# Two more pieces of raw weights loaded at the opening of an attention-plus-two-MLP kernel

## The chip, the cores and the metric

The kernel runs on one core of one Trainium2 chip. The metric is the device time of one execution in microseconds (us), lower is better; a time is the median of several runs.

## What is computed

Attention over pooled keys and values, then an MLP with ELU, then an MLP with a normalised softmax gate; all in float32, with products accurate to about float32.

```
k_p, v_p = k, v averaged over groups of 8 rows          # 8 batches, 8 heads, 576 rows of 64
x   = softmax(q @ k_p.T / 8) @ v_p                      # 4608 tokens x 512
h   = x @ w_in;  g = where(h > 0, h, exp(h) - 1)        # w_in 512 x 2048
x   = g @ w_out                                         # w_out 2048 x 512
h   = x @ moe2_w_in;  solu = h * softmax(h)             # 512 x 1024
out = layernorm(solu) * g_ln @ moe2_w_out               # 1024 x 512
```

The weights lie in memory as 64-bit words (float64); the kernel loads them as such and turns them into float32 on the chip. q, k and v are float32.

## The kernel before

**Blocks and slots.** The 4608 tokens form nine blocks of 512. The first MLP runs block by block; for each block, 16 slots f go through the hidden units, 128 a slot: 12 matmuls h1 (`m_h1`, L455), the ELU on VectorE (L466, L467), and 12 matmuls into the output accumulators (`m_o1`, L488). Every operand is split into a high and a low part, so each product takes three matmuls. The attention of the 32 pairs of heads is spread over the slots of the blocks ahead of where it is needed (`att_half`), apart from pairs 0 to 3, which come first, in `startup`. The second MLP follows behind the ninth block.

**Weights.** They come in pieces of two columns of 128 (`("i", c)`: w_in) or two rows of 128 (`("o", c)`: w_out), c = 0, 2, ... 14, sixteen pieces in all, in the order i0, o0, i2, o2, i4, and so on. `conv_load` (L315) loads a piece as raw 64-bit words into a tile `raw`, with two transfers of 512 KB. `conv` (L329) makes float32 of it with one instruction on ScalarE (L342) and three on VectorE (L344, L346, L348); the result of a w_in piece goes to a tile `cv` and from there, by `conv_split`, to `wh` and `wl`; that of a w_out piece goes to a half of a tile `wo`. `next_conv` converts the next piece of a list `cq` and loads the next of a list `lq`; it is called through the slots of block 0 until the list is empty, so all conversion is done by the end of block 0.

**The opening.** `startup` computes pairs 0 to 3 and converts i0 and o0. Of each pair: reduce k over groups of eight (`K`, L138), scores (L163), maximum and subtraction (L179, L188), exponential on ScalarE (L193), sum, reciprocal and product (`att_soft`, L200 to L204), transposes on TensorE (L214, L219) and copies on ScalarE (L215, L221), product with v (L238), and the split of the result into `xh` and `xl` (L251, L252), which the first h1 matmul needs beside `wh` and `wl`.

**Tiles and queues.** Three rings of tiles of 8 KB a partition matter here. Ring `x` has six: raw words, `xh`, `xl`. Ring `w` has eight, for `wh` and `wl` of four groups of slots; in the opening it holds four tiles with k and q of pairs 0 to 3 and a tile `kz`. Ring `wo` has four, for `wo`; in the opening it holds two tiles with v. All transfers are issued by SP, in one queue. A k tile of a later pair (tag `k`) has one buffer: k5's transfer waits until k4 is reduced.

**The order on each engine.** The text of the program gives the order of priority; a scheduler then lays the instructions of each engine in a queue of its own at build time, by its own idea of when operands are ready. What stands in a queue runs in that order on the chip.

Of the kernel before, what the change touches and what calls it, by code (L numbers as in the profile page):

```python
# [11 lines left out]
I64 = mybir.dt.int64  # L12
# [6 lines left out]
def kernel(  # L19
# [16 lines left out]
    P = 128  # L36
# [11 lines left out]
    sb = ctx.enter_context(tc.tile_pool(name="sb", bufs=2))  # L48
# [72 lines left out]
    def att_setup(i, what="kv"):  # L121
        b, p = units[i]
        early = i < NP
        if early:
            k_t, _, v_t = st["kq", p]
            if "kz" not in st:
                kz = sb.tile([P, 4, 512], F32, name="kz", tag="w", bufs=8)
                nc.vector.memset(kz[:, :, 0:2 * SK], 0.0)
                st["kz"] = kz
            kp = st["kz"][:, p, 0:2 * SK]  # L130
            vt = st["kz"][0:SK, p, 2 * SK:2 * SK + P]
        else:
            k_t, v_t = st.pop(("ld", i))
            kp = kpbd[i % 2]
            vt = p1.tile([SK, P], F32, name=f"vt{i}", tag="vt")
        if "k" in what:
            kr = p1.tile([P, SK], F32, name=f"kr{i}", tag="kr", bufs=1)
            nc.vector.tensor_reduce(kr, k_t.rearrange("p (s t) -> p s t", t=POOL), axis=AX, op=ALU.add)  # L138
            cpy = nc.vector.tensor_copy if early else nc.scalar.copy
            cpy(kp[0:64, 0:SK], kr[0:64, :])  # L140
            cpy(kp[64:128, SK:2 * SK], kr[64:128, :])
        if "v" in what:
            vr = p1.tile([SK, P], F32, name=f"vr{i}", tag="vr", bufs=1)
            if early:
                pool_tree(vr, v_t)
            else:
                nc.vector.tensor_reduce(vr, v_t, axis=AX, op=ALU.add)
            nc.scalar.mul(vt, vr, 1.0 / POOL)
        st["kp", b, p] = (kp, vt)
# [4 lines left out]
    def att_scores(i, banks):  # L154

        kp, vt = st["kp", units[i][0], units[i][1]]
        q_t = st.pop(("q", i))
        st["sv", i] = []
        for t0 in (0, 3):
            s = next(banks)  # L160
            ts = QT[t0:t0 + 3]
            for t, o in enumerate(ts):
                nc.tensor.matmul(  # L163
                    s[:, t * 2 * SK:(t + 1) * 2 * SK], q_t[:, o:o + P], kp, start=True, stop=True
                )
            m = 2 * len(ts)
            st["sv", i].append((2 * t0, m, s[:, 0:m * SK].rearrange("p (a k) -> p a k", k=SK)))
            yield
        st["a", i] = (p1.tile([P, NG, SK], F32, name=f"es{i}", tag="es", bufs=3), vt)

    def att_max(i):
        es, vt = st["a", i]
        mx = p1.tile([P, NG], F32, name=f"mx{i}", tag="mx", bufs=4)
        summed = NP <= i < NEXP
        if summed:
            st["sm", i] = p1.tile([P, NG], F32, name=f"sm{i}", tag="mx", bufs=4)
        for g0, m, sv in st.pop(("sv", i)):
            mxs = mx[:, g0:g0 + m]
            nc.vector.tensor_reduce(mxs, sv, axis=AX, op=ALU.max)  # L179
            if summed:  # L180
                nc.vector.tensor_scalar(mxs, mxs, -1.0 / (8 * POOL), None, op0=ALU.mult)
                for g in range(m):
                    nc.scalar.activation(
                        es[:, g0 + g, :], sv[:, g, :], AF.Exp, bias=mx[:, g0 + g:g0 + g + 1],
                        scale=1.0 / (8 * POOL), accum_out=st["sm", i][:, g0 + g:g0 + g + 1],
                    )
            else:
                nc.vector.tensor_tensor(es[:, g0:g0 + m, :], sv, bc(mxs, m), op=ALU.subtract)  # L188

    def att_exp(i):  # L190
        es, vt = st["a", i]
        if ("sm", i) not in st:
            nc.scalar.activation(es, es, AF.Exp, scale=1.0 / (8 * POOL))  # L193
# [31 lines left out]
    def att_V(i, banks):  # L225


        b, p = units[i]
        es, vt = st.pop(("a", i))
        a = st.pop(("aT", i))  # L230
        j = b * S // 512
        n = 512 * (j + 1) - b * S
        st["pv", i] = []
        for o, w, blk, at in ((0, n, j, b * S - 512 * j), (n, S - n, j + 1, 0)):
            pv = next(banks)
            for h in range(2):
                d = slice(64 * h, 64 * h + 64)
                nc.tensor.matmul(pv[d, 0:w], vt[:, d], a[:, h, o:o + w], start=True, stop=True)  # L238
            st["pv", i].append((pv[:, 0:w], blk, slice(at, at + w)))
# [24 lines left out]
    def double():  # L264
        t = ps.tile([P, 2, 512], F32, name="at2", tag="A")
        yield t[:, 0]
        yield t[:, 1]
# [34 lines left out]
    for j in range(NBLK):  # L302
        i = ((starts[j] + sizes[j] - 1) // S) * NP + NP - 1
# [8 lines left out]
    wraw, wcv, wh, wl, wo = {}, {}, {}, {}, {}  # L312
    w2, o2h, o2l = {}, {}, {}

    def conv_load(key):  # L315
        kind, i = key
        raw = sb.tile([P, 2, 512], I64, name="raw", tag="x", bufs=6)
        for a in range(2):
            c, d = i + a, raw[:, a, :]
            if kind == "i":  # L320
                nc.sync.dma_start(
                    out=d.rearrange("p (k f) -> p k f", k=KDM),
                    in_=w_in[:, c * P:(c + 1) * P].rearrange("(k p) f -> p k f", p=P),
                )
            else:
                nc.sync.dma_start(out=d, in_=w_out[c * P:(c + 1) * P, :])
        wraw[key] = raw

    def conv(key):  # L329
        kind, i = key  # L330
        raw = wraw.pop(key).bitcast(U32).rearrange("p a f -> p (a f)")
        hw, lw = raw[:, 1::2], raw[:, 0::2]
        if kind == "o":
            if i % 4 == 0:
                wo[i // 4] = sb.tile([P, 4, 512], F32, name="wo", tag="wo", bufs=4)
            w2 = wo[i // 4][:, i % 4:i % 4 + 2, :]
        else:
            w2 = sb.tile([P, 2, 512], F32, name="cv", tag="cv", bufs=2)
        w = w2.rearrange("p a f -> p (a f)")
        wu = w.bitcast(U32)  # L340
        wcv[key] = w2
        nc.scalar.activation(w, hw.bitcast(F32), AF.Abs, scale=2.0**-112)  # L342
        yield
        nc.vector.tensor_scalar(wu, wu, 3, None, op0=ALU.logical_shift_left)  # L344
        yield
        nc.vector.scalar_tensor_tensor(wu, lw, 29, wu, op0=ALU.logical_shift_right, op1=ALU.bitwise_or)  # L346
        yield
        nc.vector.scalar_tensor_tensor(wu, hw, 0x80000000, wu, op0=ALU.bitwise_and, op1=ALU.bitwise_or)  # L348
        yield
# [295 lines left out]
    lq = list(order)  # L645
    cq = list(order)

    def next_load():
        if lq:
            conv_load(lq.pop(0))  # L650
# [16 lines left out]
    def startup():  # L667

        ci, co = conv(("i", 0)), conv(("o", 0))

        def K(i):
            att_setup(i, "k")

        def S_(i):
            for _ in att_scores(i, double()):
                pass

        def M(i):
            att_max(i)
            att_exp(i)  # L680

        def V(i):
            att_setup(i, "v")
            att_V(i, double())

        def T(i):
            att_T(i, 0)
            att_T(i, 1)

        K(0)  # L690
        S_(0)
        K(1)
        S_(1)
        M(0)
        K(2)
        M(1)
        S_(2)
        K(3)
        att_soft(0)
        T(0)  # L700
        M(2)
        S_(3)
        att_soft(1)
        T(1)
        M(3)
        V(0)
        next(ci)
        att_soft(2)
        T(2)
        V(1)  # L710
        att_x(0)
        next(ci)
        next(ci)
        att_soft(3)
        T(3)
        att_x(1)
        V(2)
        next(ci)
        conv_split(("i", 0))
        att_x(2)  # L720
        V(3)
        att_x(3)
        for _ in co:
            pass
        conv_split(("o", 0))

    with tc.manual_schedule():
        for i in range(NP):
            att_load(i, "kq")
        att_load(0, "v")  # L730
        att_load(1, "v")
        conv_load(("i", 0))
        att_load(2, "v")
        att_load(3, "v")
        conv_load(("o", 0))
        startup()
    del cq[:2], lq[:2]
    next_load()
    nload[0] = NP
    step = 4 * NP  # L740
    while nload[0] < NP + 2:
# [124 lines left out]
```

## Time and profile before

| | |
|---|---|
| median of 3 runs | 1401.44 us (1400.01 to 1404.63) |
| the profiled execution's own time | 1404.09 us |
| its span | 1402.3 us |
| TensorE matmul busy | 1344.3 us, 96% |
| VectorE (DVE) busy | 863.5 us, 62% |
| ScalarE (ACT) busy | 649.1 us, 46% |
| GpSimd (POOL) busy | 302.9 us, 22% |
| mean granted TensorE clock | 0.985 |

The span is counted from the first to the last instruction; start times in the rows are from its beginning. A bracket in a row of the timeline gives the time that the engine sat idle ahead of the instruction and what ended it. SPq is SP's queue; a transfer's row there is its issue, not its run.

### The profile page before, as it was taken

The numbers are of one execution on the slowest core, as the hardware profiler recorded it, in microseconds if no ns is written. First come the engines' busy times: TensorE is split into PE (matmuls) and PEld (weight loads), VectorE is DVE, ScalarE is ACT, GpSimd is POOL, SyncE is SP. The second block draws the span as 40 slices with busy tenths as digits, with TensorE's granted clock in tenths as the row PEclk, the third lists the DMA queues.
The fourth block names the chain that finished last, engine by engine and source line by source line (L and its number), as shares of the span: only waits on it lengthen the run. The fifth ranks groups of instructions, "written<-read, shape, count | busy, mean of one in ns | idle before, by whom it ended". The sixth has DMA issues, their size and how long they took to land.

```text
span 1402.3 us, 16772 instructions
## 1 busy us (share of the span) xinstructions
PE 1344.3 (96%) x6260; PEld 1070.7 (76%) x6260; DVE 863.5 (62%) x1470; ACT 649.1 (46%) x1257; POOL 302.9 (22%) x245
## 2 busy tenths in 40 slices
PE   4698999999999999999999999999899999999998
PEld 3366778878788788787787777887688888787876
DVE  6699966566566466555554375643857575656653
ACT  2555544444444344444444343433645464555443
POOL 2245422222322222222223132221000000000000
PEclk7699999999999999999999999999999999999999
DMA  7355321122022122121010141535111101110000
GB/s 211 105 173 174 113 94 64 35 94 73 26 94 73 28 92 73 35 64 35 27 38 1 33 177 61 188 142 207 41 53 53 41 36 53 53 53 24 26 20 38
DMA packets 48336, 105.93 MB, mean 76 GB/s; under 512 B 4608, under 2 KB 12800, under 8 KB 46848
## 3 DMA queue, kind: packets, MB, share of 16 engines
q1 hardware_dynamic: 48256, 104.88, 22.5%
q8 instruction: 49, 0.80, 0.2%
q14 instruction: 31, 0.25, 0.1%
HBM read 74.45 MB, written 30.41 MB: 75 GB/s over the span
## 4 chain that ended last, share of the span: by engine, by line
PE 75%; DVE 14%; DMA 5%; ACT 3%; issue 2%; POOL 0%; SPq 0%; DVEq 0%; ACTq 0%
PE o L488 24%; PE h L455 24%; PE po L632 9%; PE xy L549 7%; DVE e L599 2%; PE z L549 2%; PE at L163 2%; DMA x1r<-x1d 2%; PE at L238 2%; PE pt L214 2%; DVE sc L595 1%; DMA k<-in_k 1%; ACT ha L605 1%; DMA raw<-in_w 1%; PE pt L617 1%
## 5 line engine op out<-in xcount | busy, mean ns | idle before, releaser
L437 POOL TENSOR_TENSOR wol<-wo,woh 128x512 fp32r<-128x512 f32 x144 | 205.2, 1425 | 535.2 <-ACT woh L436 535.2
L455 PE MATMUL h<-xh,wh 128*128 128x512 f32 x576 | 236.8, 411 | 1.0 <-ACT wh L362 1.0
L488 PE MATMUL o<-gh,woh 128*128 128x512 f32 x576 | 228.0, 396 | 7.4 <-ACT woh L436 5.0
L488 PE MATMUL o<-gh,wol 128*128 128x512 f32 x576 | 227.2, 394 | 1.8 <-POOL wol L437 1.8
L455 PE MATMUL h<-xl,wh 128*128 128x512 f32 x576 | 227.1, 394 | 0.0
L455 PE MATMUL h<-xh,wl 128*128 128x512 f32 x576 | 225.9, 392 | 0.5 <-POOL wl L363 0.5
L632 PE MATMUL po<-o,dhl 128*128 128x512 f32 x864 | 209.4, 394 | 2.0 <-ACT dhl L620 2.0
L466 DVE TENSOR_SCALAR e<-e 128x512 f32<-128x512 f32 x144 | 62.9, 437 | 220.7 <-ACT e L460 220.4
L632 PEld LDWEIGHTS po<-o,dhl 128*128 128x128 f32 x864 | 161.3, 188 | 37.3 <-ACT dhl L620 2.5
L460 ACT ACTIVATE e<-h 128x512 f32<-128x512 f32 x144 | 86.1, 598 | 214.1 <-PE h L455 214.1
L469 ACT CAST gh<-e 128x512 fp32r<-128x512 f32 x144 | 89.6, 622 | 154.1 <-DVE e L467 154.1
L455 PEld LDWEIGHTS h<-xh,wh 128*128 128x128 f32 x576 | 108.6, 189 | 34.7 <-issue 13.6
L488 PEld LDWEIGHTS o<-gh,woh 128*128 128x128 f32 x576 | 108.9, 189 | 33.0 <-ACT woh L436 5.5
L488 PEld LDWEIGHTS o<-gh,wol 128*128 128x128 f32 x576 | 108.9, 189 | 25.8 <-POOL wol L437 2.3
L455 PEld LDWEIGHTS h<-xl,wh 128*128 128x128 f32 x576 | 108.4, 188 | 24.9
L455 PEld LDWEIGHTS h<-xh,wl 128*128 128x128 f32 x576 | 108.9, 189 | 21.9 <-POOL wl L363 1.4
L436 ACT CAST woh<-wo 128x512 fp32r<-128x512 f32 x144 | 89.4, 622 | 35.4 <-PE o L488 32.4
L607 POOL TENSOR_TENSOR sc<-sc,mhalf 128x1 f32<-128x1 f32 x36 | 21.5, 596 | 389.9 <-DVE sc L606 389.9
L467 DVE TENSOR_TENSOR e<-e,h 128x512 f32<-128x512 f32 x144 | 98.9, 687 | 3.7
L549 PE MATMUL xy<-T,xh 128*128 128x512 f32 x216 | 78.0, 402 | 1.6 <-DVE ha L572 0.9
L635 ACT ACTIVATE ot<-po,sc 128x512 f32<-128x512 f32 x36 | 24.7, 687 | 86.1 <-PE po L632 79.0
L204 POOL TENSOR_TENSOR es<-es,sm 128x720 f32<-128x720 f32 x28 | 41.2, 1472 | 100.5 <-DVE sm L202 92.4
(562 smaller groups left out, 2207.0 us busy)
## 6 DMA issues: line engine op xcount, KB each, us to landing
raw<-in_w SPq DMA_DIRECT2D x48, 512.0 KB
v<-in_v SPq DMA_DIRECT2D x32, 288.0 KB
x1d<-x1s SPq DMA_DIRECT2D x9, 1024.0 KB
x1r<-x1d SPq DMA_DIRECT2D x9, 1024.0 KB
out<-ot SPq DMA_DIRECT2D x36, 256.0 KB
k<-in_k SPq DMA_DIRECT2D x28, 288.0 KB
q<-in_q SPq DMA_DIRECT2D x28, 288.0 KB
w2d<-cv SPq DMA_DIRECT2D x14, 512.0 KB
```

The lines of the kernel that those rows point to most:

```text
L163: nc.tensor.matmul(s[:, t * 2 * SK:(t + 1) * 2 * SK], q_t[:, o:o + P], kp, start=True, stop=True)
L204: eng.tensor_tensor(es, es, bc(sm, NG), op=ALU.mult)
L436: nc.scalar.copy(oh, t[:, f % 4, :])
L437: nc.gpsimd.tensor_tensor(ol, t[:, f % 4, :], oh.bitcast(F32), op=ALU.subtract)
L455: nc.tensor.matmul(h[:, 0:n], a[g][:, kk, fo:fo + P], x[j][:, kk, 0:n], start=(i == 0), stop=(i == 3 * KDM - 1))
L460: nc.scalar.activation(e[:, 0:n], h[:, 0:n], AF.Exp)
L466: nc.vector.tensor_scalar(e[:, 0:n], e[:, 0:n], 1.0, 1.0, op0=ALU.min, op1=ALU.subtract)
L467: nc.vector.tensor_tensor(e[:, 0:n], e[:, 0:n], h[:, 0:n], op=ALU.max)
L469: nc.scalar.copy(gh[:, 0:n], e[:, 0:n])
L488: nc.tensor.matmul(acc, a[:, dm * P:(dm + 1) * P], x[:, 0:n], start=(f == 0 and m == 0), stop=(f == NF - 1 and m == 2))
L549: nc.tensor.matmul(bank, x[:, o:o + P], w[:, y + k, :], start=(start and m == 0), stop=(stop and m == 5), skip_group_check=True,)
L632: nc.tensor.matmul(po, a[:, c, :], w[c // 4][:, c % 4, :], start=(m == 0), stop=(m == 3 * NC2 - 1))
```

## The change

The list of loads moves by two pieces. The raw words of i2 and o2 are loaded in the opening, right behind those of o0: i2 into a tile of ring `w`, o2 into a tile of ring `wo`, and the load that followed the opening (`next_load()`) goes. The list of conversions stays as it was, so loads run two pieces further ahead of conversions. Lines of the changed kernel from `conv_load` on are two higher, those behind the opening three.

```diff
     def conv_load(key):
         kind, i = key
-        raw = sb.tile([P, 2, 512], I64, name="raw", tag="x", bufs=6)
+        tag, bufs = {("i", 2): ("w", 8), ("o", 2): ("wo", 4)}.get(key, ("x", 6))
+        raw = sb.tile([P, 2, 512], I64, name="raw", tag=tag, bufs=bufs)
...
         conv_load(("o", 0))
+        conv_load(("i", 2))
+        conv_load(("o", 2))
         startup()
-    del cq[:2], lq[:2]
-    next_load()
+    del cq[:2], lq[:4]
     nload[0] = NP
```

What it does to the queues is more than the diff shows. On SP's queue, from the second pair of v tiles (v22) on; raw_105, raw_110, raw_113 and raw_116 are the words of i0, o0, i2 and o2; k4, q4, v4 and q5 belong to pairs 4 and 5. Before:

```order
L112 DMA v22_97<-in_v 72x1024 x2
L326 DMA raw_110<-in_w2 128x512 x2
L107 DMA k4_351<-in_k 128x576
L109 DMA q4_353<-in_q 128x576
L112 DMA v4_352<-in_v 72x1024
L109 DMA q5_359<-in_q 128x576
L107 DMA k5_357<-in_k 128x576
```

And now:

```order
L112 DMA v22_97<-in_v 72x1024 x2
L328 DMA raw_110<-in_w2 128x512 x2
L323 DMA raw_113<-in_w1 128x4x128 x2
L328 DMA raw_116<-in_w2 128x512 x2
L107 DMA k4_354<-in_k 128x576
L109 DMA q4_356<-in_q 128x576
L112 DMA v4_355<-in_v 72x1024
L109 DMA q5_362<-in_q 128x576
L107 DMA k5_360<-in_k 128x576
```

Four transfers of 512 KB stand ahead of k4. On ACT, from the exponential of pair 0 (es0) on, before:

```order
L193 ACTIVATE es0_125<-es0_125 128x720
L193 ACTIVATE es1_136<-es1_136 128x720
L215 COPY a0_169<-pt0_0_170 72x512
L215 COPY a0_169<-pt0_1_176 72x512
L221 COPY a0_169<-pr0_182 72x2x64
L193 ACTIVATE es2_159<-es2_159 128x720
```

And now; L344 is L342 of before, here for o2, and kpbd0, kpbd1 belong to pairs 4 and 5:

```order
L193 ACTIVATE es0_131<-es0_131 128x720
L344 ACTIVATE wo_348<-raw_116 128x1024
L193 ACTIVATE es1_142<-es1_142 128x720
L140 COPY kpbd0_77<-kr4_367 64x72
L141 COPY kpbd0_77<-kr4_367 64x72
L215 COPY a0_175<-pt0_0_176 72x512
L140 COPY kpbd1_78<-kr5_550 64x72
L141 COPY kpbd1_78<-kr5_550 64x72
L215 COPY a0_175<-pt0_1_182 72x512
```

The conversion of o2 stands ahead of the exponential of pair 1. On DVE, from the subtraction of pair 1 (es1) on, before:

```order
L179 TENSOR_REDUCE mx1_147<-at2_130 128x4
L188 TENSOR_TENSOR es1_136<-at2_130,mx1_147 128x288
L138 TENSOR_REDUCE kr3_160<-kq3_100 128x72
L140 COPY kz_113<-kr3_160 64x72
L141 COPY kz_113<-kr3_160 64x72
L200 TENSOR_REDUCE sm0_164<-es0_125 128x10
L201 TENSOR_SCALAR sm0_164<-sm0_164 128x10
L202 RECIPROCAL sm0_164<-sm0_164 128x10
L204 TENSOR_TENSOR es0_125<-es0_125,sm0_164 128x720
L179 TENSOR_REDUCE mx2_186<-at2_153 128x6
```

And now; L346, L348 and L350 are L344, L346 and L348 of before:

```order
L179 TENSOR_REDUCE mx1_153<-at2_136 128x4
L346 TENSOR_SCALAR wo_348<-wo_348 128x1024
L188 TENSOR_TENSOR es1_142<-at2_136,mx1_153 128x288
L138 TENSOR_REDUCE kr3_166<-kq3_100 128x72
L348 SCALAR_TENSOR_TENSOR wo_348<-raw_116,wo_348 128x1024
L140 COPY kz_119<-kr3_166 64x72
L141 COPY kz_119<-kr3_166 64x72
L200 TENSOR_REDUCE sm0_170<-es0_131 128x10
L138 TENSOR_REDUCE kr4_367<-k4_354 128x72
L201 TENSOR_SCALAR sm0_170<-sm0_170 128x10
L350 SCALAR_TENSOR_TENSOR wo_348<-raw_116,wo_348 128x1024
L202 RECIPROCAL sm0_170<-sm0_170 128x10
```

The three steps for o2 and the reduction of k4 have moved in among the work of pairs 0 and 1; those for i2 follow further down, ahead of the rest of i0's. From the reduction of pair 9's v (vr9, the 180th instruction of DVE in both) all queues are the same.

## Rows read from the trace of the kernel before

**Rows 1.** The page: busy time and share of the span.
```profile
PE 1344.3 (96%) x6260; PEld 1070.7 (76%) x6260; DVE 863.5 (62%) x1470; ACT 649.1 (46%) x1257; POOL 302.9 (22%) x245
```
**Rows 2.** Stretches (us), length, then each engine's busy time, PEclk, DMA share, GB/s.
```profile
0.00:155.00 155.00, 112.08 (x488) 82.33 (x488) 128.93 (x171) 79.36 (x207) 58.51 (x51) 0.87 0.55 170
145.00:155.00 10.00, 7.11 (x32) 4.79 (x30) 9.97 (x14) 7.01 (x28) 3.06 (x3) 1.00 0.62 214
155.00:180.00 25.00, 24.99 (x123) 19.28 (x124) 21.72 (x29) 12.53 (x27) 13.49 (x9) 1.00 0.12 36
```
**Rows 3.** Waits of DVE from 13 to 156 us: total, times, longest.
```profile
DVE xl L252 <- ACT xh L251: 6.5, 5, 3.4
DVE kr L138 <- DMA k<-in_k: 5.8, 2, 4.7
DVE vr L147 <- DMA k<-in_k: 2.9, 1, 2.9
DVE wo L344 <- ACT wo L342: 1.2, 1, 1.2
DVE gl__940 L476 <- ACT gh L469: 0.7, 1, 0.7
DVE gl__468 L476 <- ACT gh L469: 0.6, 1, 0.6
DVE cv L344 <- ACT cv L342: 0.5, 1, 0.5
DVE mx L179 <- PE at L163: 0.5, 1, 0.5
```
**Rows 4.** Timeline of the opening: start, duration, instruction.
```profile
13.70 0.46 DVE L188 TENSOR_TENSOR es<-at,mx 128x288 f32<-128x288 f32 x1
...
27.97 0.75 DVE L138 TENSOR_REDUCE kr<-k 128x72 f32<-128x576 f32 x1 [4.67 <-DMA k<-in_k]
...
50.44 1.16 PE L455 MATMUL h<-xh,wh 128*128 128x512 f32 x2 [0.97 <-ACT wh L362]
```
**Rows 5.** Timeline of SP's queue: start of the issue and its length.
```profile
13.84 0.33 SPq L107 DMA_DIRECT2D k<-in_k  x1
...
20.98 0.33 SPq L109 DMA_DIRECT2D q<-in_q  x1
28.75 7.81 SPq L107 DMA_DIRECT2D k<-in_k  x3
```
**Rows 6.** Stretches of three us in the opening, columns as in Rows 2.
```profile
6.00:9.00 3.00, 2.98 (x12) 2.99 (x13) 1.32 (x4) 0.00 (x0) 0.00 (x0) 1.00 1.00 376
9.00:12.00 3.00, 1.78 (x10) 1.56 (x8) 2.88 (x7) 0.80 (x1) 0.00 (x0) 1.00 1.08 262
12.00:15.00 3.00, 1.46 (x10) 1.28 (x10) 2.87 (x7) 0.81 (x1) 1.11 (x1) 1.00 1.07 278
15.00:18.00 3.00, 0.00 (x0) 0.00 (x0) 2.85 (x6) 0.00 (x0) 2.76 (x5) 0.84 1.08 282
18.00:21.00 3.00, 1.78 (x9) 1.35 (x10) 2.93 (x5) 0.58 (x1) 0.31 (x1) 0.50 0.97 218
```
**Rows 7.** DMA issues: transfers and size of one.
```profile
raw<-in_w SPq DMA_DIRECT2D x48, 512.0 KB
...
k<-in_k SPq DMA_DIRECT2D x28, 288.0 KB
```
**Rows 8.** Timeline: conversion steps on ACT and DVE in block 0.
```profile
58.92 1.17 ACT L342 ACTIVATE wo<-raw 128x1024 f32<-128x1024 f32 x1
58.98 0.69 DVE L344 TENSOR_SCALAR cv<-cv 128x1024 uint32<-128x1024 uint32 x1 [0.54 <-ACT cv L342]
...
72.15 1.88 DVE L344 TENSOR_SCALAR wo<-wo 128x1024 uint32<-128x1024 uint32 x1
74.06 1.22 DVE L346 SCALAR_TENSOR_TENSOR wo<-raw,wo 128x1024 uint32<-128x1024 uint32 x1
75.32 1.22 DVE L348 SCALAR_TENSOR_TENSOR wo<-raw,wo 128x1024 uint32<-128x1024 uint32 x1
```

## The prediction

> **What bounds the kernel now.** I began with the page's busy time. TensorE (PE) is busy for 96% of the span [rows 1], so what a change is worth is how much idle time of PE it adds or takes away. The stretches tell where that idle time lies: before 155 us PE is busy for 112.08 of 155, behind it 24.99 of 25 [rows 2]. In the same first stretch VectorE (DVE) is busy for 128.93 us, and in its last ten us for 9.97, while PE has 7.11 [rows 2]. So DVE bounds the time up to about 155 us, by attention of the first pairs, ELU and conversion, and PE everything behind it. The waits of DVE from 13 us on are the third view: 18.7 us in eight kinds, the sum of the totals of [rows 3], with the transfer of k4 the largest single one, 4.67 us at 27.97 [rows 3, 4]. The fourth is the order of the queues, since that is what the change moves.
>
> One thing makes the sum simple. DVE executes the same instructions in both kernels, and from vr9 on all queues are equal. So the whole difference is made by that point, and it is the change in DVE's idle time up to there (and in how long its instructions take), as long as DVE is the bound.
>
> **What it removes, adds and moves.** No arithmetic is added. The four transfers of i2 and o2 come earlier, in the opening; the later loads move up by two pieces; conversion of o2 and i2 moves from block 0 into the opening. None of the two early tiles waits for a free place: ring `wo` has two tiles with v and the first `wo` beside o2, ring `w` seven tiles beside i2 until i2 is converted.
>
> *The stall.* ACT now has o2's conversion second, behind the exponential of pair 0, and DVE has the first step on its result ahead of es1's second part. That part starts at 13.70 before [rows 4]. Now everything behind it waits on both engines until o2's words have landed and ACT has converted them, and PE with them, for the transposes of pair 0 need DVE's product. When do they land? Before, the transfers of k4, q4, v4 and q5 are issued between 13.84 and 20.98 [rows 5]; each takes its turn when an older one has landed. In the new order these four turns belong to i2 and o2. k4 landed at 27.97, where DVE's wait for it ended [rows 4]: by then all of the opening up to o0 was there. In front of the end of o2 now lie four transfers of 512 KB more, and k4's 288 KB no longer [rows 7]: 2.10 MB less 0.295 is 1.80 MB. From 9 to 18 us, when the DMA engines are as full as they get, they move 262, 278 and 282 GB/s [rows 6], 274 on average. That is 1.80 / 0.274 = 6.6 us, so o2 lands at 34.5. The bounds are the fastest and slowest of the full rows, 376 and 218 GB/s [rows 6]: 4.8 and 8.3 us, 32.8 and 36.2. I take the average, since i2 comes in pieces of 1 KB as i0 did, and i0 was under way in these rows. ACT's step takes 1.17 [rows 8]. DVE goes on at 34.5 + 1.17 = 35.7 in place of 13.70: **+22.0 us** of idle time (20.3 to 23.7).
>
> A page speaks of a faster rate: the Trainium skill, DMA: Bandwidth & Descriptors, section Bandwidth, has 1 MB from memory arriving at 341 GB/s. By it the 1.80 MB would take 5.3 us and the sum below would be an estimated 1.3 us less. The rows above show less in this opening, and are used.
>
> *What the stall takes in.* k4 lands 288 KB behind o2, some 1.1 us later at 274 GB/s, and its reduction now stands seven DVE instructions behind the point where DVE resumes, so its wait of 4.67 goes. k5's, the other part of the 5.8 of that row [rows 3], goes too: its transfer can start when k4 is reduced, and a conversion step, the product of pair 0 and a maximum now lie between. **-5.8**. The waits of DVE on ACT's first conversion step, 1.2 and 0.5 [rows 3], come from words that landed late or a full ACT; with loads two pieces ahead I count them as gone: **-1.7**. The wait of 2.9 at vr and those of xl on xh, 6.5, hang on POOL, ACT and PE in the chain behind pairs 2 and 3, which is ordered as before; they stay. Bounds: only k4's 4.7 goes, or all 18.7.
>
> *The conversions themselves.* In block 0 o2's three steps took 1.88, 1.22 and 1.22 [rows 8]; the first ran beside POOL's subtractions. In the opening POOL waits too, and I take 0.69 for it, what the same step took for i2, undisturbed [rows 8]: **-1.2** (0 to -1.2). i2's three take the same as before. The work on DVE is only moved, so it gives no more than this. That conversions are out of the way when the first slots run is of use to PE, which can run slot 2 while o0 is converted, but DVE is what bounds that stretch, and PE's gain there is waited away later.
>
> *SP.* k4, q4, v4, q5 are issued four turns later; their readers stand behind the stalled instructions, so this costs nothing, as long as DVE resumes after o2. Loads of i4 and o4 wait for the same releases of ring `x` as i2 and o2 did (the last steps of i0 and o0), and are needed two pieces later: nothing.
>
> *Sum:* 22.0 - 5.8 - 1.7 - 1.2 = **+13.3 us**. Against the profiled execution's own 1404.09 that is 1417.4; this execution was 2.65 above the median of its three runs, 1401.44, so the median to expect is **1414.7 us**. The first h1 matmul, at 50.44 before [rows 4], shifts by more than the end does: by the stall less k4's and k5's waits, plus the two conversions now ahead of it, 0.69 + 1.22 + 1.22 = 3.1 us each [rows 8]: 22.0 - 5.8 + 6.2, so about 73 us; block 0 gives the conversions back.
>
> **The rivals.** *The idle time is nearly all made good.* After a long stall nothing is late any more, and DVE never waits again. For it: 18.7 us of waits are there to be taken in [rows 3]. Against it: 9.4 of them, xl and vr, end with work that is itself behind the stall. It gives 22.0 - 18.7 - 1.2 = +2.1, 1403.5.
>
> *New waits in the opening.* The reductions of k5 and k6 now stand among the instructions of pairs 0 to 2 on DVE, and ACT copies k5's result between two copies of pair 0, so both queues now wait for a chain of load, reduce, load that they had behind them before. SP's three issues k5, k6, k7 take 7.81 us in one row [rows 5], so a link of it takes about (7.81 - 0.33) / 2 = 3.7. I find enough work between the links to cover one; where both are uncovered by three quarters, it costs 5.6 more: +18.9, 1420.3. A late o2, 36.2, gives +1.7 of the same sign.
>
> *The other side: faster.* If the transfers did fit into the time when DVE waits for k4 anyway, o2 would be there at 27.97, the stall would be 27.97 + 1.17 - 13.70 = 15.4, and with all waits taken in the sum is 15.4 - 18.7 - 1.2 = -4.5, 1396.9. The point from which it decides is a landing at 32.4, where the stall equals 18.7 + 1.2; at 1.80 MB past 27.97 that needs 406 GB/s, and the best row has 376 [rows 6]. The Trainium skill's first page, Trainium Kernel Development and Optimization, Best Practices, asks for DMA to be overlapped with compute, by which earlier loads would be such a gain; here nothing needed them early, and what was moved with them is an instruction that waits.
>
> *It does not do what it says:* the queues leave no room for that; what they leave open is the length of the wait.
>
> **How the numbers follow.** The forecast (+6 to +17) has 0.68, new waits 0.18, idle time made good 0.10, faster 0.04. 0.3% is 4.2 us, about what a measurement of this kernel can tell from no change. Slower by more takes in the first two and a fifth of the third: 0.88; the same most of the third, 0.08; faster 0.04. The range, from +3.6 to +20.6, leaves out most of the third case, the fourth, and the far end of the second: 1405 to 1422.
>
> **What would show it.** In the profile of the changed kernel: ACT's L344 second in the opening, starting near 34.5 behind a wait of about 22 us that a transfer of raw words ends; DVE's L346 behind it, near 35.7; no wait of DVE for k4; the first h1 near 73; PE as busy as before behind the point where the queues are equal, and that point some 13 us later. It is wrong if ACT's wait ends before 30, if DVE is idle for over 6 us in new places behind it, or if PE is not full from block 1 on.

## The result and the profile after

The changed kernel takes **1415.05 us** (median of 5 runs, 1413.57 to 1415.88); the kernel before, in 5 runs beside it, 1401.44 (1400.01 to 1404.63). The ratio is 1.0092, with a 95% interval of 1.008 to 1.0104: slower by 0.9%. The forecast was 1414.7, inside a range of 1405 to 1422. The end came out on the point; some of the steps to it did not, and this section shows which.

The profiled execution took 1413.57 us, its span is 1411.8. The page's busy times of the kernel after, to set against [rows 1]:

```profile
PE 1341.8 (95%) x6260; PEld 1071.2 (76%) x6260; DVE 856.9 (61%) x1470; ACT 648.7 (46%) x1257; POOL 303.4 (21%) x245
```

Its stretches, with the columns of [rows 2]:

```profile
0.00:155.00 155.00, 102.94 (x464) 77.73 (x465) 118.97 (x166) 75.26 (x189) 58.78 (x50) 0.85 0.52 166
145.00:155.00 10.00, 10.00 (x52) 8.38 (x51) 9.91 (x13) 5.15 (x17) 5.77 (x4) 1.00 0.67 239
155.00:180.00 25.00, 22.83 (x110) 17.51 (x109) 19.73 (x26) 13.97 (x37) 9.23 (x7) 1.00 0.15 46
```

In the first 155 us PE is busy 9.1 us less than before, and DVE 10.0 us less. The timeline of the opening of the kernel after shows where (the brackets as in [rows 4]):

```profile
28.39 1.12 ACT L344 ACTIVATE wo<-raw 128x1024 f32<-128x1024 f32 x1 [16.87 <-DMA raw<-in_w]
...
29.54 0.69 DVE L346 TENSOR_SCALAR wo<-wo 128x1024 uint32<-128x1024 uint32 x1 [16.12 <-ACT wo L344]
30.15 0.45 DVE L188 TENSOR_TENSOR es<-at,mx 128x288 f32<-128x288 f32 x1
...
33.55 0.74 DVE L138 TENSOR_REDUCE kr<-k 128x72 f32<-128x576 f32 x1
...
36.71 1.90 PE L214 MATMUL pt<-ident,es 128*72 128x128 f32 x8 [23.37 <-DVE es L204]
...
63.95 1.02 PE L457 MATMUL h<-xh,wh 128*128 128x512 f32 x2 [0.98 <-ACT wh L364]
```

ACT stands at o2's conversion until the raw words have landed, DVE behind ACT for 16.12 us, and PE behind DVE for 23.37. The second part of es1, at 13.70 before [rows 4], runs at 30.15. k4's reduction no longer waits. The waits of DVE in the kernel after, 13 to 156 us (against [rows 3]):

```profile
DVE wo L346 <- ACT wo L344: 16.1, 1, 16.1
DVE xl L252 <- ACT xh L251: 4.4, 3, 3.4
DVE vr L147 <- ACT kz L148: 2.9, 1, 2.9
DVE cv L346 <- ACT cv L344: 2.6, 3, 1.3
DVE e L468 <- ACT e L462: 1.4, 1, 1.4
DVE gl__673 L478 <- ACT gh L471: 1.1, 1, 1.1
DVE kr L138 <- DMA k<-in_k: 0.2, 1, 0.2
```

What filled the wait stands in the stretches of the kernel after (the transfers of i2 and o2 are issued from 12.33 to 19.6):

```profile
18.00:21.00 3.00, 0.00 (x0) 0.00 (x0) 0.00 (x0) 0.00 (x0) 0.00 (x0) 0.50 1.05 292
21.00:24.00 3.00, 0.00 (x0) 0.00 (x0) 0.00 (x0) 0.00 (x0) 0.00 (x0) 0.50 1.06 372
24.00:27.00 3.00, 0.00 (x0) 0.00 (x0) 0.00 (x0) 0.00 (x0) 0.00 (x0) 0.50 0.98 366
```

For nine us no engine but DMA does anything.

**A second pair of profiles.** Both kernels were profiled once more on one chip; these executions lie nearer to their medians (1401.0 and 1415.21 us), and the accounts below use them.

> The kernel before once more, for a second profile. If k4's landing at 27.97 us was ordinary, DVE waits 4 to 5 us for it again; if the transfers of the first profile were slow, k4 lands near 25 us, the wait is under 2 us and the store of block 0 is issued 2 to 4 us earlier than at 186.44. 1400 to 1404 us.

Measured for before: 1401.14 (1397.56 to 1404.47, 10 runs), ratio to the other runs of the same kernel 0.9989 [0.9973, 1.0005]. The second of the two cases came: k4's wait was shorter (2.28 us, a little over the 2 expected) and the store of block 0 was issued at 182.99, 3.5 us earlier.

> The changed kernel once more, for a second profile. ACT's wait for o2's words ends at 28 to 30 us again, and the store of block 0 is issued 7 to 12 us later than in the kernel before; 1413 to 1416 us.

Measured for after: 1414.83 (1412.37 to 1416.57, 4 runs), ratio 1.0081 [1.0055, 1.0107]. The store is 11.5 us later than in this pair's kernel before, inside the expected 7 to 12; ACT's wait ended at 27.37, before the expected 28 to 30. In the timeline of the second profile of before, k4 is there 3.4 us earlier than in [rows 4]:

```profile
24.59 0.75 DVE L138 TENSOR_REDUCE kr<-k 128x72 f32<-128x576 f32 x1 [2.28 <-DMA k<-in_k]
```

And in that of after, o2 is there 1.0 us earlier than in the first:

```profile
27.37 1.12 ACT L344 ACTIVATE wo<-raw 128x1024 f32<-128x1024 f32 x1 [15.95 <-DMA raw<-in_w]
```

So the kernel differs from execution to execution in its opening by some us: a landing read from one profile carries an error of that size.

**Where the time went, by PE.** The store of block 0's result is a mark that ends the opening. It is issued at 182.99 before and at 194.48 after: +11.5. The time from 13 us to this store, before (PE's busy time is the first number behind the length):

```profile
13.00:182.99 169.99, 136.86 (x613) 100.80 (x612) 147.24 (x189) 93.03 (x236) 70.74 (x50) 0.90 0.44 143
```

And after:

```profile
13.00:194.48 181.48, 136.69 (x613) 102.01 (x613) 141.34 (x189) 93.86 (x236) 69.63 (x50) 0.84 0.42 133
```

PE's idle time is 33.1 and 44.8 us, so all of the 11.5 is idle time of PE. The waits of PE from 13 to 200 us, the largest, before:

```profile
PE pt L214 <- DVE es L204: 9.2, 3, 5.1
PE at L238 <- ACT kz L148: 6.1, 3, 3.5
PE o L488 <- ACT woh L436: 5.0, 1, 5.0
PE o L488 <- ACT gh L469: 2.2, 1, 2.2
```

After:

```profile
PE pt L214 <- DVE es L204: 29.0, 3, 22.5
PE at L238 <- ACT kz L148: 3.7, 3, 1.9
PE o L490 <- DVE gl__587 L478: 2.1, 1, 2.1
```

The stall adds 19.8 at the transposes. Something comes back: the waits for o2's high part (`woh`, 5.0) and for `gh` (2.2) are gone, and `kz` costs 2.4 less, together about half of the wait. Not all of this is the early conversion. The wait for `woh` is gone in every profile in which both pieces are converted among the opening's work (after, e6, e8) and is 3.1 in e1 and e2, where they come behind it. But `gh` and `kz` wait little (0.3 and 2.9) in e1 too, which has a stall and no early conversion.

The rest lies behind block 0. Up to the store of block 7 little is added (888.26 and 900.19, +11.9); the span ends at 1399.2 and 1413.4, +14.2. More than half of the last 2.3 is made in the second MLP between one load and the first store of the output. SP's queue in the second profile of before:

```profile
985.44 0.57 SPq L513 DMA_DIRECT2D x1r<-x1d  x1
...
1006.34 14.79 SPq L636 DMA_DIRECT2D out<-ot  x2
```

And of after:

```profile
997.33 0.57 SPq L515 DMA_DIRECT2D x1r<-x1d  x1
...
1019.69 14.76 SPq L638 DMA_DIRECT2D out<-ot  x2
```

That is 20.90 and 22.36 us, +1.5. PE's waits there are the same in both, 2.7, 2.1 and 0.9 us (973 to 1023 us before, 985 to 1035 after); what differs is the granted clock, which falls in this stretch after the change (last section). It falls a second time near the end, where a group of 45 matmuls (PE `po`) takes 11.77 us and took 10.57.

### The profile page after: what moved, and what is told of

The parts are those of the page before. It is cut to its first block, busy times and chain, and to the rows that moved or that the text cites. A ratio compares the mean times of both kernels' runs of the same rounds, so it can differ in the third digit from the quotient of the medians.

```text
span 1411.8 us, 16765 instructions
## 1 busy us (share of the span) xinstructions
PE 1341.8 (95%) x6260; PEld 1071.2 (76%) x6260; DVE 856.9 (61%) x1470; ACT 648.7 (46%) x1257; POOL 303.4 (21%) x245
## 4 chain that ended last, share of the span: by engine, by line
PE 75%; DVE 14%; DMA 4%; ACT 3%; issue 2%; SPq 1%; POOL 1%; DVEq 0%; ACTq 0%
PE o L490 25%; PE h L457 25%; PE po L634 9%; PE xy L551 7%; DVE e L601 2%; PE z L551 2%; DMA x1r<-x1d 2%; PE at L163 2%; PE at L238 2%; DMA raw<-in_w 2%; PE pt L214 2%; DVE sc L597 1%; ACT ha L607 1%; PE pt L619 1%; DVE wo L350 1%
## 5 line engine op out<-in xcount | busy, mean ns | idle before, releaser
L457 PEld LDWEIGHTS h<-xh,wh 128*128 128x128 f32 x576 | 108.7, 189 | 35.8 <-issue 13.6
L457 PEld LDWEIGHTS h<-xh,wl 128*128 128x128 f32 x576 | 109.0, 189 | 21.2 <-POOL wl L365 0.6
L214 PE MATMUL pt<-ident,es 128*72 128x128 f32 x256 | 40.4, 286 | 34.1 <-DVE es L204 30.7
L204 POOL TENSOR_TENSOR es<-es,sm 128x720 f32<-128x720 f32 x28 | 42.0, 1499 | 107.6 <-DVE sm L202 91.8
```

Source lines behind the costliest of these rows:

```text
L204: eng.tensor_tensor(es, es, bc(sm, NG), op=ALU.mult)
L214: nc.tensor.transpose(pt[0:SK, t * P:(t + 1) * P], es[:, 2 * t + h, :], ident)
L457: nc.tensor.matmul(h[:, 0:n], a[g][:, kk, fo:fo + P], x[j][:, kk, 0:n], start=(i == 0), stop=(i == 3 * KDM - 1))
```

## The experiments

Two theories. **Wait**: the loss is that two queues stand in order behind an instruction whose operand is the last thing to land in the opening. Rivals: **transfers** (four more transfers of 512 KB in the opening cost the time by themselves), and **work** (conversions ahead of the first slots delay them). Each experiment was run beside the kernel before, which had a median of 1401.83 in 29 runs beside e1 to e4, and 1402.3 in 29 runs beside e6 and e8 and the second profiles. Ratios are to it.

### e1: early loads kept, conversion of i2 and o2 behind pair 3

`xa` and `xd` are the last copy on ACT and the last split on DVE of the pair; `issue_after` makes the scheduler place the instructions inside it behind that one in the queues and adds no wait of its own.

```diff
+            if i == NP - 1:
+                gate["xa"], gate["xd"] = xa, xd
...
-            for _ in conv(cq[0]):
-                pass
+            if cq[0][1] == 2:
+                with tc.issue_after(gate["xa"]), tc.issue_after(gate["xd"]):
+                    for _ in conv(cq[0]):
+                        pass
...
```

> The early loads stay, but the conversions of i2 and o2 are queued on ACT and DVE behind the last split of pair 3 (xh, xl). The scheduler then has the reduction of k4 on DVE ahead of the product of pair 0. Theory 'wait' (a queue stands behind a transfer that has not landed): the stall only changes its name; DVE reaches k4's reduction near 15.5 us and waits until k4, which comes behind o2, has landed near 30: 14 to 15 us, of which 4.7 were there before. 1408 to 1415 us. Rival 'work' (the two conversions in the opening cost it): with them gone from there, 1400 to 1404 us.

Measured: 1417.31 us, ratio 1.011 [1.009, 1.0131], no faster than the change and above the expected 1408 to 1415. The work theory falls: with the conversions out of the opening nothing is won. In the timeline of e1 another instruction has taken the place of o2's conversion:

```profile
30.87 0.75 DVE L138 TENSOR_REDUCE kr<-k 128x72 f32<-128x576 f32 x1 [14.55 <-DMA k<-in_k]
```

k4's transfer stands behind the four, and its reduction still stands ahead of the work of pairs 0 and 1.

### e2: e1, and k4's reduction behind pair 3 too

```diff
-    att_setup(NP)
+    with tc.issue_after(gate["xd"]):
+        att_setup(NP)
```

> As the run before this one, and the set-up of pair 4 (reduction of k4) also queued behind the last split of pair 3 on DVE. Theory 'wait': nothing in the opening waits for a late transfer any more; no wait of DVE over 4 us between 13 and 45 us, the first h1 matmul at 43 to 47 us, and the time below the kernel before by the 4.7 us it spent on k4 or a little more: 1393 to 1399 us. Rival 'transfers' (2 MB more in the opening cost it by themselves, whatever the order): 1408 to 1416 us.

Measured: 1401.54 us, ratio 0.9997 [0.9984, 1.0011]. All four early transfers are still there, in the same place of SP's queue, and the loss is gone: 15.8 us less than e1 by moving the set-up of one pair. That refutes the transfers theory and shows the wait. The gain that I expected beyond that (1393 to 1399 us) didn't come. A wait took the place of k4's, in the waits of DVE in e2:

```profile
DVE xl L252 <- ACT xh L251: 15.5, 8, 5.0
```

xl waited 6.0 in the second profile of before. My guess was that the work which stood among pairs 0 to 3 had filled these waits; e6 and e8 test that.

### e3: the kernel before, with k4's reduction behind pair 3

The edit is that of e2 on the kernel before, which still converts i2 and o2 in block 0.

```diff
-    att_setup(NP)
+    with tc.issue_after(gate["xd"]):
+        att_setup(NP)
```

> The kernel before, with only the set-up of pair 4 queued behind the last split of pair 3 on DVE; no early loads. Theory 'wait': it saves the 4.7 us wait for k4: 1395 to 1399 us. If the early loads of i2 and o2 are worth something of their own, the run with them and with the same queue is faster than this one by more than 2 us; if not, the two are within 2 us of each other.

Measured: 1405.24 us, ratio 1.0023 [1.001, 1.0036]: slower, not faster. The profile is of its fastest execution, 1401.39 us. In it DVE's wait for k4 (4.67 in [rows 3]) is gone, and xl waits 13.8 us in its place, as in e2. So k4's wait was not there to be won in this way; what makes the median slower than before the profile does not show. Between e3 and e2 lie the early loads with conversion after pair 3: 3.7 us in favour of the loads, though the two intervals touch.

### e4: o2 alone early

```diff
-        tag, bufs = {("i", 2): ("w", 8), ("o", 2): ("wo", 4)}.get(key, ("x", 6))
+        tag, bufs = {("o", 2): ("wo", 4)}.get(key, ("x", 6))
...
-        conv_load(("i", 2))
         conv_load(("o", 2))
         startup()
-    del cq[:2], lq[:4]
+    del cq[:2], lq[:2], lq[1]
+    next_load()
```

> Only o2 is loaded early; i2 is loaded behind the opening, as before. The scheduler then has o2's conversion on ACT behind the copies of pair 1, and on DVE, with k4's reduction, behind the sum of pair 2, where the queues arrive near 26 us. Theory 'wait': o2 and k4 have landed by 25 to 28, so the wait is 0 to 3 us in place of 4.7: 1396 to 1402 us. Rival 'transfers': half of the added bytes, half of the loss, 1406 to 1410 us. Rival 'work': one of two conversions in the opening, 1406 to 1410 us.

Measured: 1399.76 us, ratio 0.9993 [0.9978, 1.0008]. With half the bytes ahead of it the wait is 0.88 us. The scheduler, too, lays o2's conversion further back here, on ACT behind the copies of pairs 0 and 1, so this run changes two things at once. The timeline of e4:

```profile
25.32 1.12 ACT L344 ACTIVATE wo<-raw 128x1024 f32<-128x1024 f32 x1 [0.88 <-DMA raw<-in_w]
...
26.01 0.75 DVE L138 TENSOR_REDUCE kr<-k 128x72 f32<-128x576 f32 x1 [0.44 <-DMA k<-in_k]
```

The words land 2 to 3 us earlier than after the change, and the stall is shorter by 15: most of the loss hangs on where in the queue the conversion stands when its words come.

### e6 and e8: early loads, conversion as filling

If e2 lost its gain by idle gaps around pair 3, then conversion should stand in these gaps: behind pair 3's exponential on ACT (`sa`) and pair 2's product on DVE (`sd`). In e6 k4's reduction goes behind `sd`, in e8 behind pair 0's last split.

```diff
+            if i == 3:
+                gate["sa"] = last
...
+        if i == 2:
+            gate["sd"] = last
...
+            if cq[0][1] == 2:
+                with tc.issue_after(gate["sa"]), tc.issue_after(gate["sd"]):
+                    for _ in conv(cq[0]):
+                        pass
...
```

> Both early loads; the conversions of i2 and o2 and the set-up of pair 4 queued on DVE behind the product of pair 2 (es2) and on ACT behind the exponential of pair 3. DVE then comes to k4's reduction near 27 us, ACT to o2's conversion later still. Theory 'wait': the words have landed by then but for a wait of 3 to 4 us for k4, the conversions fill the 15 us that DVE spent in the opening waiting for xh when both were queued last, and block 0 has two conversions less: 1393 to 1400 us. Rival 'early conversion is of no use': like the run with both queued last, 1400 to 1404 us.

> As the run before this one, with pair 4's set-up queued behind the first split of pair 0 on DVE, so that k4's reduction comes behind i2's conversion. Theory 'wait': no wait over 2 us for a transfer is left; equal to the run before this one or up to 4 us faster: 1391 to 1398 us. Rival 'early conversion is of no use': 1400 to 1404 us.

Measured: e6 1400.01 us, ratio 0.998 [0.9967, 0.9993]; e8 **1399.06** us, ratio 0.997 [0.9959, 0.9982], so 3.2 us below the kernel before and 16 below the change. Both are at or above the top of what I expected (1400 and 1398), and in e8 one wait for a transfer, 2.8 us, is over the 2 that I allowed. Both intervals lie below 1; e6 and e8 can't be told apart. The gain is small: e8's ratio is 0.3%, the bound that the prediction gave for no change. The waits of DVE in e8, 13 to 156 us:

```profile
DVE vr L147 <- ACT kz L148: 2.9, 1, 2.9
DVE kr L138 <- DMA k<-in_k: 2.8, 1, 2.8
DVE xl L256 <- ACT xh L255: 2.0, 3, 0.9
```

xl waits 2.0 instead of 15.5 in e2, by the same loads. PE's waits for `woh` are gone as they are after the change, while its waits at the transposes are 14.9 us (29.0 after the change, 9.2 before), and block 0's store goes out at 178.80 (182.99 before). No run has k4's reduction where e8 has it without the early loads, so how much of the small gain is theirs stays open.

## Why the prediction was right

*The mechanism* held as written: ACT's conversion of o2 second in the opening, its words the last to land, DVE and PE behind it; e1 and e2 have the same early loads and conversions and differ in the place of one set-up, and with the wait the loss goes. *The sum* was +13.3 us, and medians give +13.6 (1415.05 less 1401.44). But its terms were wrong in both directions, and the sum was right because they offset: the mechanism was understood, the number was luck. The second pair of profiles, 14.2 us apart, gives for DVE (idle and busy time from 13 us to vr9; the third line is what is left of the idle time):

| term | predicted, us | measured, us |
|---|---|---|
| stall at o2 | +22.0 | +15.2 |
| waits for k4, k5 (k6) | -5.8 | -4.1 |
| other idle time of DVE | -1.7 | +4.0 |
| DVE's busy time | -1.2 | -6.2 |
| behind vr9 | 0 | +5.4 |
| sum | +13.3 | +14.3 |

By steps:

**The landing of o2, 34.5, was wrong:** 28.39 and 27.37, and so was **the stall, +22.0:** DVE was idle for 16.1 and 15.2 us. This is the step that failed, and by the prediction's own sign (wrong if ACT's wait ends before 30). Two things went into it. I started from k4's landing at 27.97, which was a slow one; from 24.59, as in the second profile, my own sum would have given 31.2. The other 3.8 us to 27.37 come from the rate: I put 1.80 MB behind the landing of k4 at 274 GB/s. The bytes were about right: up to those landings the second profile of before moved 263 GB/s x 24.59 us = 6.5 MB, after 299 x 27.37 = 8.2 MB, 1.7 more. The rate was not. The stretch from 13 us to k4's landing, before:

```profile
13.00:24.59 11.59, 6.46 (x31) 5.36 (x30) 8.93 (x18) 3.51 (x7) 4.08 (x5) 0.71 0.97 279
```

From 13 us to o2's landing, after:

```profile
13.00:27.37 14.37, 0.24 (x2) 0.03 (x1) 0.32 (x1) 0.00 (x0) 2.98 (x5) 0.54 1.02 338
```

The DMA share of 1.02 says that the queue did not run low. From 12 to 21 us the first profile of after moves 288, 292 and 292 GB/s, near my 274; in the two stretches behind that, by when all of i2 and o2 is issued, 372 and 366. That engines stood idle there is not the reason: e2 moves 376 and 366 GB/s in the same two stretches with DVE busy for 2.24 and 2.83 us of three. In e4, without i2, 329 and 359 GB/s are there from 18 and 21 us on, so it seems to be o2's words that move faster; that was not tried by itself. My row was one of other transfers. The page that I set against it, the Trainium skill, DMA: Bandwidth & Descriptors, section Bandwidth, has 341 GB/s for 1 MB; the 338 over the whole stretch lies near it, and my row did not. Counted from 27.97, it too would have given a landing near 33.

**-5.8, the waits for k4 and k5, held** in the first pair: 5.8 became 0.2. In the second profile of before there were only 4.1 to lose.

**-1.7, the waits on ACT's first conversion step, was wrong:** in the same pair of rows 1.7 became 2.8 (2.6 at `cv`, 0.2 at `wo` behind the stall).

**-1.2, o2's first step, held for that step** (0.69, 1.22 and 1.22) and was mis-sized for DVE as a whole. From 13 us up to vr9, from where the queues are equal, DVE in the second pair was busy for 130.37 us before (vr9 at 161.11) and 124.13 after (at 169.93): -6.2. The groups of steps by line, before:

```profile
L346 DVE SCALAR_TENSOR_TENSOR wo<-raw,wo 128x1024 uint32<-128x1024 uint32 x8 | 15.2, 1906 | 0.2
L344 DVE TENSOR_SCALAR wo<-wo 128x1024 uint32<-128x1024 uint32 x8 | 10.1, 1267 | 1.2 <-ACT wo L342 1.2
```

After:

```profile
L348 DVE SCALAR_TENSOR_TENSOR wo<-raw,wo 128x1024 uint32<-128x1024 uint32 x8 | 12.3, 1532 | 0.1
L346 DVE TENSOR_SCALAR wo<-wo 128x1024 uint32<-128x1024 uint32 x8 | 6.2, 781 | 15.4 <-ACT wo L344 15.4
```

These two groups alone are 6.8 us shorter (the three of w_in are 2.3 us longer). That is 4.5 of the 6.2. The long first step of [rows 8], 1.88 us, stood beside POOL's product (L204, 71.64 to 73.48 in the trace), not beside subtractions as I wrote. Of the 16 first steps of the conversions in the second pair, seven took over 1 us before and two after, and each of these nine stood beside POOL's work for over half of its time; but one short step stood beside it throughout. So the cause is likely what POOL does at the same time, and no run tried it.

**"The whole difference is made by vr9" held for the opening; "DVE is the bound" was wrong.** PE's idle time from 13 us to vr9 is 33.1 before and 44.8 after, as much as up to block 0's store. Behind vr9 PE is full; from vr9 to the store, before:

```profile
161.11:182.99 21.88, 21.88 (x109) 17.42 (x108) 16.87 (x27) 11.06 (x23) 5.29 (x4) 1.00 0.18 55
```

And after:

```profile
169.93:194.48 24.55, 24.55 (x122) 19.76 (x121) 17.21 (x27) 12.05 (x25) 5.84 (x4) 1.00 0.16 49
```

DVE comes to vr9 only 8.8 us later (idle time +15.1, busy time -6.2; 4.8 in the first pair), where I had some 13, but PE then has 122 matmuls left to the store in place of 109. So it is PE that ends the opening, 11.5 us later, and DVE's shorter work is no gain. The table's 5.4 behind vr9 are 2.7 of this, 0.4 up to block 7, and 2.3 of the second MLP with its lower clock, which the prediction had at nothing. Summing DVE's idle time gave 8.8 of the opening's 11.5; PE's account, by idle time up to the store of a block, is the one that closes.

**First h1 near 73, was wrong** by the failed term: 63.95, and 64.76 in the second profile. In the second pair it is 17.7 later (47.04 before), and my own sum with the measured terms gives 15.2 - 4.1 + 6.2 = 17.3. Block 0 then gives back 6.2 (the store +11.5), and 6.0 of 13.5 in the first pair (186.44 and 193.90), where I had 9.

*The rivals.* Idle time made good (+2.1) did not happen: xl and vr kept waiting (4.4 and 2.9 us; [rows 3] puts vr's wait down to k's transfer, both profiles of after to ACT). New waits of k5 and k6 did not come: DVE waits 0.2 us for k in all. Faster needed o2 there by 32.4; it was there at 28.39, so this condition *was* met, and the change was slower all the same. The point was worked out with all 18.7 us of waits taken in; of waits other than the stall, 28.7 - 16.1 = 12.6 us are left in the rows of after.

## What to carry to other kernels

Loading early cost nothing here that could be measured (e2, ratio 0.9997); an instruction that reads the early load, laid by the scheduler at the head of a queue where everything else stands in order, costs the wait until the load has landed (15 to 16 us of DVE, and 7.5 and 11.5 us at the store of block 0 in the two pairs of profiles). Read for each queue which instruction has the latest operand, and keep it behind the work that is ready, as e2 does by one small edit against e1, or use it to fill gaps that you see in the waits, as e8 does. Compare two kernels' waits in the same stretch of the program and not at the same time, for all that follows a stall is shifted. And close the account on the engine that ends the stage, here PE: the sum over another engine came out right only because 11.8 us of error one way met 12.8 the other way.

## What the runs showed of the hardware

The opening's transfers differ between executions of one kernel: k4's wait ended at 27.97 and 24.59 us, with 244 and 279 GB/s from 13 us to there.

The granted clock fell at the start of the second MLP in four of ten profiles, after a pause of PE of 2.1 us that all ten have. The two stretches in which it does in the first profile of after, at 0.57, where 0.50 is the lower level (1.2 GHz) and 1.00 the upper (2.4 GHz):

```profile
1006.00:1008.00 2.00, 1.96 (x9) 1.86 (x10) 2.00 (x6) 1.92 (x4) 0.50 (x1) 0.57 0.01 4
1008.00:1010.00 2.00, 2.00 (x8) 1.52 (x7) 1.49 (x5) 0.76 (x2) 0.83 (x2) 0.57 0.00 0
```

The second profile of before, in the stretches at the same place of the program:

```profile
994.00:996.00 2.00, 1.44 (x10) 1.35 (x11) 2.00 (x6) 1.40 (x3) 0.00 (x0) 1.00 0.01 4
996.00:998.00 2.00, 2.00 (x11) 1.43 (x10) 2.00 (x7) 2.00 (x5) 0.91 (x2) 1.00 0.00 0
```

It fell there in both profiles of after, in e6 and in e8, so in just the kernels that convert both pieces among the opening's work, and not in either of before, nor in e1 to e4; why stays open. Since e8 is the fastest and e1 the slowest, it is at most a small part of the loss. In the four us shown PE starts 9 + 8 = 17 matmuls after, and 10 + 11 = 21 before; at some 0.4 us each, that is an estimated 1 to 2 us. The marks agree: from the load at 985.44 of before to the first store of the output it is 20.9 to 21.2 us in the six profiles where the clock stays, and 22.3 to 22.4 in the four where it falls.

Near the end it fell in four profiles too, but not the same four: the second of after, e1, e4 and e6, after a pause of 1.46 us that before has as well. The 45 matmuls behind it take 11.5 to 11.9 us there, and 10.6 in both profiles of before. So of the 14.2 us between the second pair's spans over 2 are clock, while in the first pair (9.5 us between the spans) only the first fall is there; how much of the medians' 13.6 is clock can't be told from two profiles.
